# An mLSTM cell and a multiplicative FFN on one core: the division by the denominator on GpSimd, the output gate in one VectorE pass

## The chip, the cores and the metric

The kernel runs on 1 core of a Trainium2 chip. The core has five engines with a queue of instructions each: TensorE (PE in the profile; PEld are its weight loads), VectorE (DVE), ScalarE (ACT), GpSimd (POOL) and SyncE (SP, here used to issue DMAs). Each engine works through its own queue in order and waits on semaphores for the others. The metric is the device time of one execution in microseconds (us); lower is better.

## The reference

Two blocks follow each other, all in float32. The first is an mLSTM cell over 4 batches, 8 heads, 768 time steps and head size 40; the second is an FFN without an activation over the 3072 tokens.

```python
def _attn_ref(q, k, v, i_gate, f_gate, o_gate):
    ...
    for t in range(S):
        m_new = np.maximum(f_gate[:, :, t] + m, i_gate[:, :, t])
        f_stab = np.exp(f_gate[:, :, t] + m - m_new)
        i_stab = np.exp(i_gate[:, :, t] - m_new)
        m = m_new
        C = f_stab[:, :, None, None] * C + i_stab[:, :, None, None] * np.einsum('bhd,bhe->bhde', vt, kt)
        n = f_stab[:, :, None] * n + i_stab[:, :, None] * kt
        h_tilde = np.einsum('bhde,bhe->bhd', C, qt)
        nq = np.einsum('bhd,bhd->bh', n, qt)[:, :, None]
        denom = np.maximum(np.abs(nq), 1.0)
        o = 1.0 / (1.0 + np.exp(-o_gate[:, :, t]))
        y[:, :, t] = o * h_tilde / denom

def _moe_ref(x, w1, w2, w3, w_out):
    a = x @ w1
    b = x @ w2
    h = a * b @ w3
    return h @ w_out
```

The change touches the last line of the cell: `o * h_tilde / denom`.

## The kernel before

The cell is computed in chunks of 64 time steps. A unit is one batch and 128 time steps (two chunks) with all 8 heads; there are NU = 24 units, `n = 0..23`, four batches by six pairs of chunks, with time steps on the 128 partitions. For a unit, TensorE forms the scores `ss`, multiplies the masked weights `pw` with the values (`ph`), adds the part from the running state (`pi`), and makes the two state updates `pc`. A 41st column of the values is all ones, so column 40 of each head holds the denominator `nq`.

The main loop runs over steps `s = 0..31`. In step `s` the function `quarter_work(s, ...)` (from line 338) finishes the outputs of unit `s - 1` and starts unit `s`. Around it the same step puts in FFN work, so that TensorE always has something to do: the up products (`up`, `up_rest`: `pa`, `pb`, then `a_sb` and `ab`), in the first half the folding of the last two weight matrices into one (`convert`, `w3_mm`, `wp`), from step 19 on a seven-product scheme for the up products (`up_by_seven`) and later for the down products (`out_by_seven`).

The outputs of a unit are made in `outputs(n, pi, ph)` (line 420). VectorE first makes `h`, 8 heads by 41 columns per partition (L423 and, for units from 2 on, four instructions at L430). What follows is a Python generator of steps; each call of `den()` traces the next piece:

1. L438: the absolute value of column 40 into `den`, 128x8.
2. L440: maximum with 1, times 2.
3. L441: the reciprocal.
4. L443: `e = (e + 1) * den` over 128x320, where `e` is the tile `o_in`, which ScalarE has turned into tanh of half the output gate (`out_gate`, L270); L445: `y = h * e` over 128x320.

Since the sigmoid is (tanh(x/2) + 1) / 2 and `den` carries the 2, this is the reference's last line.

`quarter_work` places the calls between other VectorE work of unit `s`: after the mask of the scores (L397) come call 2, the first state update (L404, or L406 in the first four units), GpSimd's decay of the new state (L335, `decayed`), a late conversion in step 3 (`late`: L199, L200 of the weight `wr`), call 3, the second state update (L414, which reads what the decay wrote), and call 4. Units of the last pair of chunks (20 to 23) have one state update only, no second decay and no L414.

GpSimd's own queue has, per step, the decay L335, the weighting of the values `vw` for the next unit (L330), for part of the steps a copy of 64 columns of `y` (L476), two mask instructions on `pw` (L308) and the decay for the next unit (L335). In steps 16 and 17 it makes sums of weights (L659). From step 19 on it has two instructions of `up_by_seven`: L711, which finishes the set-aside sums that VectorE's L686 and L684 prepare and whose result the later L686 and L684 read, and L729, which multiplies the two factors into `ab`. From step 24 on L755 makes sums of the down weights.

From unit 15 on `y` is written to DRAM and read back in another layout by DMAs on SyncE's queue (L456, L458, L465), and VectorE turns it (L472) into the `xT` that the up products read; L666 makes the sums of `xT` that `up_by_seven` needs, and L770 the sums of `ab` for `out_by_seven`.

The order on TensorE is fixed as traced (`in_order`); that of the other engines too, from the first gate computation on, by `keep_order`, which links each instruction to the one traced before it on its engine. The `issue_after` blocks put what is traced in them behind the named instruction. The tiles `h`, `den` and `y` come from a pool with two buffers each, `a_sb` as well, and `o_in` has five.

Of the kernel before, what the change touches and what calls it, by code (L numbers as in the profile page):

```python
# [11 lines left out]
OP = mybir.AluOpType  # L12
# [4 lines left out]
def kernel(  # L17
# [26 lines left out]
    nc = tc.nc  # L44

    B, H, S, D = q.shape
    L = 64
    P = 128
# [6 lines left out]
    DM = H * D  # L55
# [21 lines left out]
    def mps(shape, name):  # L77
        pool = banks.pop(0)
        banks.append(pool)
        return pool.tile(shape, FP, name=name, tag="m")  # L80
# [10 lines left out]
    def mm(out, lhsT, rhs, start=True, stop=True):  # L91
        in_order(nc.tensor.matmul(out, lhsT=lhsT, rhs=rhs, start=start, stop=stop))  # L92
# [4 lines left out]
    def warm(n, m=4, small=0):  # L97
        bank = mps([P, 4, P], "fill")
        for _ in range(n):
            mm(bank[:, 0:m], ident, ident.unsqueeze(1).to_broadcast([P, m, P]))  # L100
        for i in range(small):
            r = halves[i % 2]
            mm(bank[r, 0, 0:L], ident[r, 0:L], ident[r, 0:L])
# [8 lines left out]
    N_DIAG = 2  # L112
# [154 lines left out]
    qT_t, kT_t, vw_t, before_t, y_t, x_t = {}, {}, {}, {}, {}, {}  # L267
# [65 lines left out]
    def decayed(new, old, n, x):  # L333
        c, b = divmod(n, B)
        nc.gpsimd.tensor_tensor(out=new, in0=old, op=OP.mult, in1=decay[:, b * NP:(b + 1) * NP, 2 * c + x:2 * c + x + 1]  # L335
                                .to_broadcast([P, NP, D1]))

    def quarter_work(s, rest, between, late):


        rest()

        def part(j, c0, n):
            return cell[j][:, :, c0:c0 + NP * n].rearrange("p x (n d) -> p x n d", d=n)

        ss, pc, pi = part(0, 0, L), part(0, NP * L, D1), part(1, 0, D1)
        ph = [cell[1][:, x, NP * D1:2 * NP * D1].rearrange("p (h d) -> p h d", d=D1) for x in range(2)]
        n = s - 1
        if 0 <= n < NU:
            pw, vt, qT = u_t.pop(n), vbuf[n % NBV], qT_t.pop(n)  # L350
            before = before_t.pop(n)
            if n < N_DIAG:
                warm(1)

            if n < N_DIAG:
                ph = mps([P, H, D1], "ph")
                for hq in range(H):
                    for r in halves:
                        mm(ph[r, hq, :], pw[r, hq, :], vt[r, hq, :])
            for hd in range(H // 2 if n >= N_DIAG else 0):  # L360
                for x, e in quarters:
                    hq = hd if x == e else hd + H // 2
                    mm(ph[x][halves[e], hd, :], pw[halves[x], hq, :], vt[halves[x], hq, :])
            for p in range(NP):
                for hip, x in quarters if n >= B else quarters[1:3]:
                    mm(pi[halves[x], hip, p, :], qT[heads[hip], p, halves[x]], before[x][heads[hip], p, :])
        den = None
        if 0 <= s - 1 < NU:
            den = outputs(s - 1, pi, ph)
            den()  # L370
            if between:
                for _ in range(3):
                    den()
                den = None
                between()
            if late:
                late()
        n, first_read = s, None
        if n < NU:
            c, b = divmod(n, B)  # L380
            kt, vw = kbuf[n % NB], vw_t.pop(n)
            ends = range(2 if c < NT2 - 1 else 1)
            first, second, after = state[b]
            before_t[n] = first, second
            state[b] = after, second, first
            kT, qT, pw = kT_t.pop(n), qT_t[n], u_t[n]
            for p in range(NP):
                for hip, x in quarters:
                    mm(ss[halves[x], hip, p, :], kT[heads[hip], p, halves[x]], qT[heads[hip], p, halves[x]])
            M = D if n else L  # L390
            for p in range(NP):
                for x, e in quarters:
                    if x in ends:
                        mm(pc[e * L:e * L + M, x, p, :], kt[halves[x], 2 * p + e, 0:M], vw[halves[x], 2 * p + e, :])
        if n < NU:
            pv = pw.rearrange("p (n two) t -> p two n t", two=2)
            first_read = nc.vector.tensor_tensor(out=pv, in0=ss, in1=pv, op=OP.mult)  # L397
        with tc.issue_after(first_read.ins) if first_read else nullcontext():
            if den:
                den()  # L400
            if n < NU:

                if c:
                    nc.vector.tensor_tensor(out=second, in0=pc[:, 0], in1=second, op=OP.add)  # L404
                else:
                    nc.vector.tensor_copy(out=second, in_=pc[:, 0])  # L406
                if len(ends) > 1:
                    decayed(after, second, n, 1)
            if late:
                late()  # L410
            if den:
                den()
            if n < NU and len(ends) > 1:
                nc.vector.tensor_tensor(out=after, in0=pc[:, 1], in1=after, op=OP.add)  # L414
            if den:
                done = den()
        return done if den else first_read

    def outputs(n, pi, ph):
        c, b = divmod(n, B)  # L420
        hs = slice(b * H, (b + 1) * H)
        h = sb.tile([P, H, D1], FP, name="h", tag="h")
        nc.vector.tensor_tensor(out=h.rearrange("p (n two) d -> p two n d", two=2), in0=pi,  # L423
                                in1=gT[:, c, hs].rearrange("p (n two) -> p two n", two=2).unsqueeze(3)
                                .to_broadcast([P, 2, NP, D1]), op=OP.mult)
        if n < N_DIAG:
            nc.vector.tensor_tensor(out=h, in0=ph, in1=h, op=OP.add)
        for x, e in quarters if n >= N_DIAG else ():
            part = h[halves[x], 0:H // 2] if x == e else h[halves[x], H // 2:H]
            nc.vector.tensor_tensor(out=part, in0=ph[x][halves[e]], in1=part, op=OP.add)  # L430

        den = sb.tile([P, H, 1], FP, name="den", tag="den")

        def steps():
            V = nc.vector
            yield V.tensor_scalar(out=den.bitcast(U32), in0=h[:, :, D:D1].bitcast(U32), scalar1=0x7FFFFFFF, scalar2=None,  # L438
                            op0=OP.bitwise_and)
            yield V.tensor_scalar(out=den, in0=den, scalar1=1.0, scalar2=2.0, op0=OP.max, op1=OP.mult)  # L440
            yield V.reciprocal(out=den, in_=den)  # L441
            e = o_t.pop(n)
            nc.vector.scalar_tensor_tensor(out=e, in0=e, scalar=1.0, in1=den.to_broadcast([P, H, D]), op0=OP.add, op1=OP.mult)  # L443
            y_t[n] = sb.tile([P, DM + REM], FP, name="y", tag="y")
            yield nc.vector.tensor_tensor(out=y_t[n][:, 0:DM].rearrange("p (h d) -> p h d", d=D), in0=h[:, :, 0:D],  # L445
                                           in1=e, op=OP.mult)

        done = steps()
        return lambda: next(done)

# [109 lines left out]
    V = nc.vector  # L560
# [7 lines left out]
    for i, r in enumerate(third):  # L568
        V.tensor_tensor_scan(out=M[r, 1:GC + 1], data0=F3[r, :, L - 1], data1=U3[r, :, L - 1], initial=M[r, 0:1],
                             op0=OP.add, op1=OP.max)  # L570
# [24 lines left out]
    for i, r in enumerate(third):  # L595
        nc.gpsimd.tensor_tensor(out=pick[r, :, i, :], in0=pair[r].to_broadcast([BH, B * NP, GC]), op=OP.mult,
                        in1=dec[r].unsqueeze(1).to_broadcast([BH, B * NP, GC]))
# [222 lines left out]
    for s in range(len(n_up)):  # L820
# [62 lines left out]
        def rest():  # L883
            for x in open_ups:
                up_rest(*x)
            if seven:
                seven[2]()
            if s == 3:
                scale_next()
                scale_next()  # L890

        def between():
            twice(1)
            weighted(2)
            rows_of_u(3)
            for _ in range(3):
                scale_next()
            for n in range(2):
                x_trans(n)
                if n == 0:  # L900
                    warm(1, small=38)
            for _ in range(3):
                convert()
            turn(2)
            block = up(*now[0])
            weighted(3)
            weights(3)
            masks(3)
            out_gate(2)
            convert()  # L910
            up_rest(*block)

        gated = None
        if s <= NU:
            gated = quarter_work(s, rest, between if s == 2 else None, convert if s == 3 else None)
        else:
            rest()
# [94 lines left out]
```

## Time and profile before

| what | value |
|---|---|
| median of 3 runs | 426.37 us (426.09 to 426.73) |
| span of the profiled execution | 425.8 us |
| ScalarE busy | 150.1 us (35%) |
| DMA traffic | 51.15 MB, mean 120 GB/s |
| L443, 24 instructions of 128x320 | 17.4 us, 0.725 us each |
| L445, 24 instructions of 128x320 | 17.0 us, 0.709 us each |
| L330, GpSimd, 24 of 128x328 | 18.3 us, 0.764 us each |
| L335, GpSimd, 40 of 128x164 | 20.0 us, 0.500 us each |
| L711 and L729, GpSimd, 22 each of 128x512 | 27.4 and 29.4 us |

The span is the time from the first to the last instruction of one profiled execution; the median is taken over separate runs and lies 0.6 us above it. Busy time is the time in which an engine works on an instruction; its waits are not in it. The granted TensorE clock is 0.996 of full speed over the span. In the rows of the timeline the first number is the start in us from the beginning of the span, the second the length, then the engine, the line, the operation, what is written and read, and the shape; a number in brackets is the idle time of that engine just before, with what ended it.

### The profile page before, as it was taken

To read this page: it belongs to the slowest core of one execution; us is meant where nothing else is said; L and a number is where in the kernel's file an instruction comes from. 1 tells how busy PE (TensorE), PEld (TensorE's weight loads), DVE (VectorE), ACT (ScalarE), POOL (GpSimd) and SP (SyncE) were. 2 spreads that over 40 slices of the span, in tenths; PEclk is the share of its full clock that TensorE was granted. 3 is DMA by queue.
4 is the path that set the end of the run, shared out by engine and by line. 5 is a ranking of instruction groups with operands and counts; after the bars stand their busy time and mean duration, and the time that the engine had idled before them with its cause. 6 is when DMAs were issued, how large, how long until landed. Compare 5 with 4: busy or idle time off the path is not lost.

```text
span 425.8 us, 13079 instructions
## 1 busy us (share of the span) xinstructions
PE 414.1 (97%) x5353; PEld 335.3 (79%) x5353; DVE 313.5 (74%) x635; ACT 150.1 (35%) x404; POOL 154.3 (36%) x211
## 2 busy tenths in 40 slices
PE   7989989999999999999999999999999999999996
PEld 4768878888688788787777778788778879888896
DVE  6676986888949779778736966596868699575971
ACT  4766865567723623630433313032311110210000
POOL 4421342233303303303307751546453587542100
PEclk9989999999999999999999999999999999999999
DMA  8999998598977776985425675756421120000001
GB/s 186 204 173 245 214 144 140 134 193 180 215 183 154 166 182 135 181 164 105 89 80 130 153 141 121 142 133 117 87 44 36 35 39 2 31 2 31 2 32 62
DMA packets 135211, 51.15 MB, mean 120 GB/s; under 512 B 109360, under 2 KB 126960, under 8 KB 135152
## 3 DMA queue, kind: packets, MB, share of 16 engines
q1 hardware_dynamic: 131552, 46.29, 53.9%
q10 hardware_dynamic: 3600, 4.03, 2.7%
q8 instruction: 42, 0.69, 0.7%
q14 instruction: 17, 0.14, 0.1%
HBM read 44.50 MB, written 5.80 MB: 118 GB/s over the span
## 4 chain that ended last, share of the span: by engine, by line
PE 53%; issue 20%; DVE 7%; POOL 7%; SPq 7%; DMA 5%; ACT 1%; POOLq 0%; DVEq 0%
PE cell L92 17%; PE pa L92 12%; PE o L92 8%; PE pb L92 8%; PE p L92 3%; POOL pw L308 3%; SPq L184 3%; DVE w3T L666 2%; PE pt L95 1%; POOL vw L330 1%; SPq L148 1%; DMA raw<-in_moe_w_dram 1%; PE fill L92 1%; POOL raw L659 1%; POOL state L335 1%
## 5 line engine op out<-in xcount | busy, mean ns | idle before, releaser
L335 POOL TENSOR_TENSOR state<-state,decay 128x164 f32<-128x164 f32 x40 | 20.0, 500 | 154.8 <-DVE state L404 129.0
L92 PE MATMUL pa<-xT,w 128*128 128x256 f32 x240 | 60.4, 382 | 0.0
L92 PEld LDWEIGHTS pa<-xT,w 128*128 128x128 f32 x240 | 44.4, 190 | 6.8 <-DVE h L430 0.4
L303 ACT ACTIVATE pw<-pw,aT 128x64 f32<-128x64 f32 x184 | 46.4, 339 | 3.2 <-ACT o_sb L741 1.9
L92 PE MATMUL pb<-xT,w 128*128 128x256 f32 x192 | 45.4, 379 | 0.0
L729 POOL TENSOR_TENSOR ab<-ab,a_sb 128x512 f32<-128x512 f32 x22 | 29.4, 1356 | 32.2 <-DVE ab L684 32.2
L92 PEld LDWEIGHTS pb<-xT,w 128*128 128x128 f32 x192 | 36.4, 190 | 5.0
L711 POOL TENSOR_TENSOR wo<-wo 128x512 f32<-128x512 f32 x22 | 27.4, 1268 | 29.8 <-DVE wo L686 29.8
L92 PE MATMUL pa<-xT,wr 64*64 64x256 f32 x384 | 37.0, 386 | 0.5 <-DVE wr L200 0.5
L92 PE MATMUL wp<-wo,w3T 128*128 128x320 f32 x128 | 35.9, 433 | 1.1 <-DVE ab L639 0.6
L308 POOL TENSOR_SCALAR_AFFINE_SELECT pw<-pw 64x512 f32<-64x512 f32 x48 | 35.8, 746 | 3.0 <-ACT pw L303 1.2
L92 PE MATMUL pb<-xT,wr 64*64 64x256 f32 x384 | 36.4, 380 | 0.0
L92 PE MATMUL cell<-w3o,ab 128*128 128x320 f32 x128 | 35.4, 432 | 0.0
L638 ACT ACTIVATE a_sb<-pa 128x512 f32<-128x512 f32 x24 | 14.3, 598 | 59.0 <-PE pb L92 59.0
L639 DVE TENSOR_TENSOR ab<-pb,a_sb 128x512 f32<-128x512 f32 x24 | 16.4, 688 | 23.2 <-ACT a_sb L638 22.8
L92 PEld LDWEIGHTS wp<-wo,w3T 128*128 128x128 f32 x128 | 23.8, 190 | 10.5 <-DVE ab L639 0.8
L92 PEld LDWEIGHTS cell<-w3o,ab 128*128 128x128 f32 x128 | 24.3, 190 | 9.5
L92 PEld LDWEIGHTS pa<-xT,wr 64*64 64x64 f32 x384 | 18.9, 132 | 15.4 <-issue 8.8
L686 DVE SCALAR_TENSOR_TENSOR a_sb<-pa,wo 128x512 f32<-128x512 f32 x12 | 8.3, 689 | 29.8 <-PE pa L92 29.8
L430 DVE TENSOR_TENSOR h<-cell,h 64x164 f32<-64x164 f32 x88 | 28.6, 326 | 1.6
L92 PE MATMUL po<-w3o,ab 128*128 128x320 f32 x96 | 26.4, 433 | 0.0
L92 PEld LDWEIGHTS po<-w3o,ab 128*128 128x128 f32 x96 | 18.1, 190 | 7.3
(180 smaller groups left out, 846.4 us busy)
## 6 DMA issues: line engine op xcount, KB each, us to landing
raw<-in_moe_w_dram SPq DMA_DIRECT2D x64, 128.0 KB, 3.4
kbuf<-in_k_dram SPq DMA_DIRECT2D x24, 160.0 KB, 4.5
v_all<-in_v_dram SPq DMA_DIRECT2D x24, 160.0 KB, 4.9
o_in<-in_o_gate_dram SPq DMA_DIRECT2D x24, 160.0 KB, 4.8
pw<-U_d SPq DMA_DIRECT2D x28, 128.0 KB, 3.5
raw<-in_moe_w_dram SPq DMA_DIRECT2D x5, 512.0 KB, 6.7
raw<-in_moe_w_out_dram SPq DMA_DIRECT2D x8, 320.0 KB, 4.1
gates<-in_k_dram SPq DMA_DIRECT2D x28, 80.0 KB, 2.5
```

What stands on the lines that cost most here:

```text
L92: in_order(nc.tensor.matmul(out, lhsT=lhsT, rhs=rhs, start=start, stop=stop))
L184: nc.sync.dma_start(out=dst, in_=src)
L303: nc.scalar.activation(out=pw[:, h, :], in_=src[:, h, :], func=AF.Exp, bias=aT[:, c, b * H + h:b * H + h + 1])
L308: nc.gpsimd.affine_select(out=pw[r], in_=pw[r], compare_op=OP.is_ge, fill=0.0, base=0, pattern=[[0, H], [1, L]], channel_multiplier=-1)
L335: nc.gpsimd.tensor_tensor(out=new, in0=old, op=OP.mult, in1=decay[:, b * NP:(b + 1) * NP, 2 * c + x:2 * c + x + 1] .to_broadcast([P, NP, D1]))
L430: nc.vector.tensor_tensor(out=part, in0=ph[x][halves[e]], in1=part, op=OP.add)
L638: nc.scalar.mul(out=a_sb, in_=pa, mul=UP ** -2)
L639: nc.vector.tensor_tensor(out=ab_t[gr][j][:, fs[0]:fs[-1] + 1, t0:t0 + a_sb.shape[-1]], in0=pb, in1=a_sb, op=OP.mult)
L666: nc.vector.tensor_tensor(out=dst, in0=p, in1=q, op=OP.subtract)
L686: nc.vector.scalar_tensor_tensor(out=out, in0=p, scalar=UP ** -2, in1=q, op0=OP.mult, op1=OP.add)
L711: aside_by.tensor_tensor(out=kept[j][:, 1:4:2], in0=kept[j][:, 1:3], in1=kept[j][:, 3:4].to_broadcast([128, 2, TH]), op=OP.add)
L729: aside_by.tensor_tensor(out=t[:, f:FO:FH, :], in0=t[:, f:FO:FH, :], in1=a, op=OP.mult)
```

## The change

For units 2 to 23 (`n >= N_DIAG`, and `N_DIAG` is 2) the two VectorE passes over 128x320 become one GpSimd pass and one VectorE pass. Right after the reciprocal GpSimd multiplies the first 40 columns of each head of `h` by the head's reciprocal, in place. VectorE's last pass is then `y = (e + 1) * h`. Units 0 and 1 keep the two VectorE passes. The tile `o_in` is no longer written by VectorE in the units that change.

In `quarter_work` the third call of `den()`, the reciprocal and with it GpSimd's multiply, moves for those units from behind the first state update, the decay and the late conversion to directly behind the second call. So on VectorE the reciprocal stands in front of L404 (or L406), and on GpSimd the multiply stands in front of the decay L335 of the same step; in steps 20 to 24, where the second decay is absent, it stands in front of the two L729. The instruction counts are 22 fewer on VectorE and 22 more on GpSimd; TensorE, ScalarE and SyncE have the same instructions in the same order. In the changed file L404 and L406 are L406 and L408, L414 is L416, L441 is L443, the new multiply is L452, the new last pass L454, and lines behind them are 8 higher.

```diff
@@ -398,6 +398,8 @@
         with tc.issue_after(first_read.ins) if first_read else nullcontext():
             if den:
                 den()
+                if s - 1 >= N_DIAG:
+                    den()
             if n < NU:
 
                 if c:
@@ -408,7 +410,7 @@
                     decayed(after, second, n, 1)
             if late:
                 late()
-            if den:
+            if den and s - 1 < N_DIAG:
                 den()
             if n < NU and len(ends) > 1:
                 nc.vector.tensor_tensor(out=after, in0=pc[:, 1], in1=after, op=OP.add)
@@ -438,12 +440,18 @@
...
-            yield V.reciprocal(out=den, in_=den)
+            done = V.reciprocal(out=den, in_=den)
             e = o_t.pop(n)
-            nc.vector.scalar_tensor_tensor(out=e, in0=e, scalar=1.0, in1=den.to_broadcast([P, H, D]), op0=OP.add, op1=OP.mult)
             y_t[n] = sb.tile([P, DM + REM], FP, name="y", tag="y")
-            yield nc.vector.tensor_tensor(out=y_t[n][:, 0:DM].rearrange("p (h d) -> p h d", d=D), in0=h[:, :, 0:D],
-                                           in1=e, op=OP.mult)
+            y, hn, all_d = y_t[n][:, 0:DM].rearrange("p (h d) -> p h d", d=D), h[:, :, 0:D], den.to_broadcast([P, H, D])
+            if n < N_DIAG:
+                yield done
+                V.scalar_tensor_tensor(out=e, in0=e, scalar=1.0, in1=all_d, op0=OP.add, op1=OP.mult)
+                yield V.tensor_tensor(out=y, in0=hn, in1=e, op=OP.mult)
+            else:
+                nc.gpsimd.tensor_tensor(out=hn, in0=hn, in1=all_d, op=OP.mult)
+                yield done
+                yield V.scalar_tensor_tensor(out=y, in0=e, scalar=1.0, in1=hn, op0=OP.add, op1=OP.mult)
```

## The prediction

> **What bounds the kernel now.** I read the busy line first, then the waits of TensorE, then the steps around the edited lines in order of time.
>
> ```profile
> PE 414.1 (97%) x5353; PEld 335.3 (79%) x5353; DVE 313.5 (74%) x635; ACT 150.1 (35%) x404; POOL 154.3 (36%) x211
> ```
>
> TensorE (PE) is busy for 414.1 of 425.8 us. VectorE (DVE) has a quarter of the span free, so taking work off it helps only where PE stands still for it. The waits of PE that end on a VectorE line this change can touch (us in total, times, longest):
>
> ```profile
> PE wp L92 <- DVE ab L639: 0.6, 1, 0.6
> PE pa L92 <- DVE wr L200: 0.5, 1, 0.5
> PE pa L92 <- DVE w3T L666: 0.4, 1, 0.4
> PE o L92 <- DVE wo L686: 0.2, 1, 0.2
> ```
>
> In time they lie at 107.8, 46.8, 242.4 and 355.9 us. Together 1.7 us: the most that relief of VectorE can return in the units that change (the wait for y at 22 us belongs to units 0 and 1, which keep their code). Now one ordinary unit, the end of step 17 (start, length, engine, line):
>
> ```profile
> 233.07 0.32 DVE L404 TENSOR_TENSOR state<-cell,state 128x164 f32<-128x164 f32 x1
> 233.31 0.20 DVE L441 RECIPROCAL den<-den 128x8 f32<-128x8 f32 x1
> 233.47 0.46 POOL L335 TENSOR_TENSOR state<-state,decay 128x164 f32<-128x164 f32 x1 [2.50 <-DVE state L404]
> 233.90 0.73 POOL L330 TENSOR_TENSOR vw<-v_all,wT 128x328 f32<-128x328 f32 x1
> 233.97 0.33 DVE L414 TENSOR_TENSOR state<-cell,state 128x164 f32<-128x164 f32 x1 [0.47 <-POOL state L335]
> 234.22 0.76 DVE L443 SCALAR_TENSOR_TENSOR o_in<-o_in,den 128x320 f32<-128x320 f32 x1
> 235.01 0.82 DVE L445 TENSOR_TENSOR y<-h,o_in 128x320 f32<-128x320 f32 x1
> ```
>
> VectorE already waits 0.47 us there for GpSimd's decay (L335). That queue is where the new multiply goes. Last, the step after the last unit (step 24) and the next:
>
> ```profile
> 335.68 2.50 POOL L729 TENSOR_TENSOR ab<-ab,a_sb 128x512 f32<-128x512 f32 x2 [4.06 <-DVE ab L684]
> ...
> 338.14 1.54 POOL L755 TENSOR_TENSOR v_all<-w3o 128x640 f32<-128x640 f32 x1
> 338.24 1.47 DVE L440 TENSOR_SCALAR den<-den 128x8 f32<-128x8 f32 x1
> 339.75 0.20 DVE L441 RECIPROCAL den<-den 128x8 f32<-128x8 f32 x1
> ...
> 342.40 2.50 POOL L711 TENSOR_TENSOR wo<-wo 128x512 f32<-128x512 f32 x2 [2.71 <-DVE wo L686]
> ...
> 343.71 0.69 DVE L686 SCALAR_TENSOR_TENSOR a_sb<-pb,wo 128x512 f32<-128x512 f32 x1
> ...
> 344.93 0.69 DVE L684 TENSOR_TENSOR ab<-pb,wo 128x512 f32<-128x512 f32 x1
> 345.07 2.94 POOL L729 TENSOR_TENSOR ab<-ab,a_sb 128x512 f32<-128x512 f32 x2 [0.17 <-DVE ab L684]
> ```
>
> From 336 to 356 us VectorE has no gap and the chain of waits runs on it (L440, L770, L472, L666, L686); at 356.12 PE's `o` product waits 0.22 us for the L686 that frees its bank. After that PE has no gap to the end. So whatever makes VectorE late here goes to the end one for one.
>
> **The change part by part.**
>
> Removed: in 22 units (2 to 23) VectorE's pass L443, mean 0.725 us, 16 us in all. Nearly all of it was behind a busy PE, so its worth is what the four waits lose, not 16 us.
>
> Added: 22 multiplies of 128x320 on GpSimd. No such row exists; the neighbours are L335 (164 columns, 0.46 us) and L330 (328 columns, 0.73), so a straight line gives 0.72 for 320. Bounds 0.46 and 1.25 (L729, 512 columns). They need the reciprocal and are queued in front of the decay L335.
>
> Ordinary units, steps 4 to 19, worked on the rows above: the reciprocal now stands before L404 and ends at about 233.4; multiply 233.45 to 234.2; L335 to 234.6; L414 starts at 234.65 (before 233.97); y to 235.7, counting 0.76 to 0.82 for a pass beside GpSimd. It ended at 235.83. So VectorE swaps a pass for a wait and gains 0.1 us; GpSimd is 0.7 us later with vw, the mask and what follows. Hidden by: vw and mask are needed a step later (10 us in the later steps, about 1 us for vw in step 3).
>
> Step 3 (unit 2): the reciprocal now stands in front of L406 and the conversion of `wr` (L199, L200) instead of behind them. That is its 0.19 us and a gap of 0.03, and PE waits for just that L200: **+0.2** (0.1 to 0.4).
>
> The wait at 107.8: y of step 8 ended at 99.6, but L199 then waited 0.63 us for ScalarE, so an earlier y is no help; GpSimd's mask slides some 0.3 us further over L199, L200 and the transpose, of which L199 took 0.62 beside the mask and 0.39 alone: **+0.1** (-0.1 to 0.3).
>
> The wait at 242.4: step 17's four L666 run beside GpSimd's L659 (1.12, 1.38, 1.49) and only the last ran nearly free (0.68). GpSimd 0.7 us later puts that last one beside L659 as well, about +0.5; y earlier gives 0.15 back. **+0.3** (-0.4, the whole wait gone, to 0.6).
>
> Steps 19 to 23: the multiply is ahead of the products L729 in the queue, and it needs the reciprocal, so L729 goes from 307.42 to about 311.6 in step 22 (reciprocal 310.75, plus 0.1, plus 0.72), likewise in 20, 21 and 23. What waits behind it: vw, mask, decay, the next L711 and PE's `cell` products of the third group, which read the finished `ab` from 313.5. First half of L729 then ends at 312.9 to 313.2: cover 0.3 to 0.6 us at least, more because the columns in question are read fourth. L711 of step 23 slides from 315.66 to about 317; its reader, L686 into a_sb at 320.18, still has room. **0** (0 to 0.5; past the cover each us costs one).
>
> Steps 24 and 25: the two L729 and the L755 now come after the multiply. L755 then no longer sits beside L440, which shrinks from 1.47 to 0.16; reciprocal ends at 338.6, multiply 338.7 to 339.4, L729 to 342.15 (2.74 for the pair, as beside VectorE's two passes in step 19), L755 to 343.7. L711 of step 25 begins there instead of at 342.40. VectorE is no earlier for it: y runs beside L729, where L445 took 1.44 in step 19, and ends near 340.8 against 341.00. L686 and L684 need the halves of L711, so L684 at 344.93 and the four L770, L472, L666 and L686 behind it all move by **+1.3**. Bounds: 0.8 (multiply at 0.46, L729 2.50, L755 1.54), 1.9 (L729 2.94, L755 1.98); and -0.2 if the pair kept its place, for then only the 0.22 us wait is left to win.
>
> [...] This case has 0.73 us for L330's 328 columns against 0.49 for an undisturbed L445 of 320, a factor of 1.5. [...]
>
> [...]
>
> Sum: 0.2 + 0.1 + 0.3 + 0 + 1.3 = 1.9 us on the profiled span of 425.8, which is 0.6 below the median of the runs (426.37); the sum is carried to the median: 428.2 to 428.3, I say **428.2**.
>
> **The rivals.**
>
> *No change to be told (about 0.2% is what a measurement of this kernel can tell).* PE covers the tail too: if the scheduler's banks give PE's `o` product at 356 some 1 us of room the trace doesn't show, only steps 3 and 17 remain, +0.3: 426.7. For it: PE has 97% and no gap between 243 and 355.9. Against it: at 356.12 PE already waits.
>
> *Faster.* VectorE's freed 16 us take away the waits at 107.8, 242.4 and 355.9 (0.58 + 0.41 + 0.22 = 1.2) less 0.2 in step 3: 425.4. One mechanism: in steps 17 and 24 a shorter VectorE chain arrives earlier; at step 24 1.3 us of L440 beside L755 vanish. It decides if GpSimd finishes L755 before 342.4, so that L711 starts when L686 lets it. Against it: 338.7 + 0.46 + 2.50 + 1.54 is already 343.2.
>
> *Much slower.* The products L729, some 4 us later in steps 20 to 23, outrun their cover at 313.5 or hold up L711: up to 2 us more, 430.2. For it: half a us of cover by my rows; against it: the columns are read fourth, 1.6 us into the block.
>
> **How the numbers follow.** Forecast 0.60, no change 0.19, faster 0.11, much slower 0.10. Faster by over 0.2%: 0.11; within: 0.19; slower: 0.70. The terms' bounds run from 0.4 (0.1 - 0.1 - 0.4 + 0 + 0.8) to 3.7 (0.4 + 0.3 + 0.6 + 0.5 + 1.9), that is 426.8 to 430.1; taking in the case of no change and its scatter the range is 426.2 to 430.1.
>
> **What would show it.** In the changed profile: the multiply near 0.72 us, 22 times; L414's wait of 0.47 grown to about 1.0; VectorE's busy time down by some 14 us at a span not shorter; L729 of steps 20 to 23 begun after the reciprocal; L711 of step 25 waiting for no VectorE row but for its own queue; PE's wait at 356 grown from 0.2 to about 1.5. I am wrong if that last wait is not longer, or if PE shows a new gap in 243 to 350.

## The result and the profile after

| | before | after |
|---|---|---|
| median (lowest to highest, runs) | 426.27 us (426.09 to 426.73, 4) | 428.47 us (428.27 to 429.39, 4) |
| time after / before, 95% interval | | 1.0063 [1.0044, 1.0082] |
| span of the profiled execution | 425.8 us | 426.4 us |

The changed kernel is slower by 1.9 to 3.5 us (the interval's ends, 0.0044 and 0.0082, times 426.27); the quotient of the two medians, 1.0052, lies within. A run more than 1.5% above the fastest of its kernel counts as slow and is left out of the ratios and of the ranges of runs given below. The spans alone would say 0.6 us, and that is misleading: wherever span and time of one execution are both known they lie 1.9 to 2.1 us apart (after: 426.4 and 428.45), so the profiled execution of before took about 427.8 us and was not a typical one.

The busy line of the page after, to be read against the one of before:

```profile
PE 413.1 (97%) x5353; PEld 334.6 (78%) x5353; DVE 303.8 (71%) x613; ACT 149.6 (35%) x404; POOL 169.4 (40%) x233
```

VectorE is busy 9.7 us less (313.5 to 303.8), GpSimd 15.1 us more. PE's own work is the same within 1.0 us. So the answer must be in the waits of PE, in the same view as before (total, times, longest, in us):

```profile
PE o L92 <- DVE wo L694: 1.4, 1, 1.4
PE pa L92 <- DVE wr L200: 1.3, 1, 1.3
...
PE cell L92 <- DVE state L416: 0.7, 2, 0.4
PE wp L92 <- DVE ab L647: 0.7, 1, 0.7
PE pa L92 <- DVE w3T L674: 0.6, 1, 0.6
```

Four of the five grew from 0.2, 0.5, nothing and 0.4; the one for `ab` stood at 0.6. Each has its place. First step 3 in the timeline of after (start, length, engine, line):

```profile
44.36 0.20 DVE L443 RECIPROCAL den<-den 128x8 f32<-128x8 f32 x1
44.64 0.72 POOL L452 TENSOR_TENSOR h<-h,den 128x320 f32<-128x320 f32 x1 [8.26 <-DVE den L443]
44.67 0.97 DVE L199 TENSOR_SCALAR wr<-raw 128x512 uint32<-128x512 uint32 x1
45.78 0.73 DVE L200 CUSTOM_DVE_ANT_0 wr<-raw,wr 128x1024 uint16<-128x1024 uint16 x1
46.57 0.43 PE L92 MATMUL pa<-xT,wr 64*64 64x256 f32 x1 [1.31 <-DVE wr L200]
```

The same place in the timeline of before:

```profile
45.99 0.42 DVE L199 TENSOR_SCALAR wr<-raw 128x512 uint32<-128x512 uint32 x1
46.54 0.73 DVE L200 CUSTOM_DVE_ANT_0 wr<-raw,wr 128x1024 uint16<-128x1024 uint16 x1
47.33 0.43 PE L92 MATMUL pa<-xT,wr 64*64 64x256 f32 x1 [0.51 <-DVE wr L200]
```

L199 starts 0.03 us after the new multiply and takes 0.97 us instead of 0.42. PE waits 0.8 us longer for what follows it.

Second, the ordinary units, in the timeline of after: the end of step 17, then of step 18.

```profile
231.45 0.72 POOL L452 TENSOR_TENSOR h<-h,den 128x320 f32<-128x320 f32 x1 [1.94 <-DVE den L443]
232.13 0.47 POOL L335 TENSOR_TENSOR state<-state,decay 128x164 f32<-128x164 f32 x1
232.55 0.74 POOL L330 TENSOR_TENSOR vw<-v_all,wT 128x328 f32<-128x328 f32 x1
232.63 0.33 DVE L416 TENSOR_TENSOR state<-cell,state 128x164 f32<-128x164 f32 x1 [1.06 <-POOL state L335]
232.87 0.76 DVE L454 SCALAR_TENSOR_TENSOR y<-o_in,h 128x320 f32<-128x320 f32 x1
...
243.94 0.72 POOL L452 TENSOR_TENSOR h<-h,den 128x320 f32<-128x320 f32 x1 [2.70 <-DVE den L443]
244.62 0.47 POOL L335 TENSOR_TENSOR state<-state,decay 128x164 f32<-128x164 f32 x1
245.12 0.33 DVE L416 TENSOR_TENSOR state<-cell,state 128x164 f32<-128x164 f32 x1 [1.07 <-POOL state L335]
...
245.50 0.70 PE L92 MATMUL cell<-w3T,raw 128*128 128x256 f32 x2 [0.38 <-DVE state L416]
```

The decay L335 stands behind the multiply, L416 waits 1.06 us for it (0.47 before). In step 17 nobody minds. In step 18 the next PE product writes the PSUM bank that L416 still reads (`pc`), and PE stands still for 0.38 us; the same in step 19 at 264.5 us (0.33). Before, the PE products ran through there: 

```profile
245.78 0.46 POOL L335 TENSOR_TENSOR state<-state,decay 128x164 f32<-128x164 f32 x1 [3.29 <-DVE state L404]
...
246.28 0.33 DVE L414 TENSOR_TENSOR state<-cell,state 128x164 f32<-128x164 f32 x1 [0.47 <-POOL state L335]
246.39 2.32 PE L92 MATMUL cell<-w3T,raw 128*128 128x256 f32 x10
```

Third, the tail, steps 24 and 25, in the timeline of after:

```profile
338.09 0.72 POOL L452 TENSOR_TENSOR h<-h,den 128x320 f32<-128x320 f32 x1 [7.09 <-DVE den L443]
338.77 2.75 POOL L737 TENSOR_TENSOR ab<-ab,a_sb 128x512 f32<-128x512 f32 x2
338.85 1.54 DVE L454 SCALAR_TENSOR_TENSOR y<-o_in,h 128x320 f32<-128x320 f32 x1 [0.84 <-POOL h L452]
...
341.48 1.54 POOL L763 TENSOR_TENSOR v_all<-w3o 128x640 f32<-128x640 f32 x1
...
342.98 2.50 POOL L719 TENSOR_TENSOR wo<-wo 128x512 f32<-128x512 f32 x2
...
344.29 0.69 DVE L694 SCALAR_TENSOR_TENSOR a_sb<-pb,wo 128x512 f32<-128x512 f32 x1 [1.25 <-POOL wo L719]
...
356.71 1.35 PE L92 MATMUL o<-w3o,ab 128*128 128x160 f32 x8 [1.43 <-DVE wo L694]
```

GpSimd works without a pause from 338.09; multiply, two products, L763, and only then L719, for which VectorE now waits 1.25 us. Before, L719 (as L711) had waited for VectorE instead. PE's wait 12 us later is 1.2 us longer.

Laid side by side, matmul by matmul, the two traces give the account. At 59 us the profiled execution of after is 2.5 us ahead. That of before had lost 1.0 us in small waits up to 23 us, 1.6 us in a slow stretch of PE at 23 to 28 us and 1.7 us at 57.6 us, in a gap that ends on no other engine; that of after 0.9 us at 43 us (it waited for `w`) and 0.9 us at 47 us. From there after falls back by 0.4 us at 108 and 144 us, where the other kernels differ from before by as much in either direction, then by 0.2 at the wait for `w3T`, 0.6 at each of the two `cell` products and 1.2 at 356 us, and it ends 0.6 us behind. With the 0.9 us at 47 us that the early lead covers, the places that touch the change sum to 3.5 us, the upper end of the measured interval.

### The profile page after: what moved, and what is told of

It reads as the page before. It is cut to its first block, busy times and chain, and to the rows that moved or that the text cites. A ratio compares the mean times of both kernels' runs of the same rounds, so it can differ in the third digit from the quotient of the medians.

```text
span 426.4 us, 13083 instructions
## 1 busy us (share of the span) xinstructions
PE 413.1 (97%) x5353; PEld 334.6 (78%) x5353; DVE 303.8 (71%) x613; ACT 149.6 (35%) x404; POOL 169.4 (40%) x233
## 4 chain that ended last, share of the span: by engine, by line
PE 77%; SPq 8%; DVE 6%; DMA 5%; issue 3%; POOL 1%; ACT 0%; DVEq 0%; POOLq 0%
PE cell L92 19%; PE pa L92 19%; PE pb L92 12%; PE wp L92 8%; PE o L92 8%; PE po L92 4%; SPq L139 3%; PE p L92 3%; DMA raw<-in_moe_w_dram 2%; SPq L184 2%; PE px L95 1%; DVE pw L778 1%; PE pt L95 1%; SPq L153 1%; DMA v_all<-in_v_dram 1%
## 5 line engine op out<-in xcount | busy, mean ns | idle before, releaser
L452 POOL TENSOR_TENSOR h<-h,den 128x320 f32<-128x320 f32 x22 | 15.9, 724 | 172.8 <-DVE den L443 172.8
L737 POOL TENSOR_TENSOR ab<-ab,a_sb 128x512 f32<-128x512 f32 x22 | 30.7, 1416 | 13.9 <-DVE ab L692 13.9
L308 POOL TENSOR_SCALAR_AFFINE_SELECT pw<-pw 64x512 f32<-64x512 f32 x48 | 34.3, 715 | 1.8 <-ACT pw L303 0.2
L719 POOL TENSOR_TENSOR wo<-wo 128x512 f32<-128x512 f32 x22 | 27.5, 1272 | 11.9 <-DVE wo L694 11.9
L694 DVE SCALAR_TENSOR_TENSOR a_sb<-pa,wo 128x512 f32<-128x512 f32 x12 | 8.3, 689 | 29.3 <-PE pa L92 29.2
```

The lines of the kernel that those rows point to most:

```text
L308: nc.gpsimd.affine_select(out=pw[r], in_=pw[r], compare_op=OP.is_ge, fill=0.0, base=0, pattern=[[0, H], [1, L]], channel_multiplier=-1)
L452: nc.gpsimd.tensor_tensor(out=hn, in0=hn, in1=all_d, op=OP.mult)
L719: aside_by.tensor_tensor(out=kept[j][:, 1:4:2], in0=kept[j][:, 1:3], in1=kept[j][:, 3:4].to_broadcast([128, 2, TH]), op=OP.add)
L737: aside_by.tensor_tensor(out=t[:, f:FO:FH, :], in0=t[:, f:FO:FH, :], in1=a, op=OP.mult)
```

## The experiments

All times are medians in us, ratios are against the kernel before, run on the same chip in the same batch. Its own median was 425.64 for the first four kernels (23 runs, 424.5 to 427.4), 426.05 for the next four (23 runs, 424.4 to 430.3) and 426.44 for the last four (24 runs, 424.7 to 428.9). Single executions scatter by more than the effects, so each kernel was also read by PE's waits in its profile. The table has both; waits in us: for `wr` at 46, for `w3T` at 242, for L416 in steps 18 and 19 (two), and in the tail.

| kernel | time | ratio, 95% interval | wr | w3T | L416 | tail |
|---|---|---|---|---|---|---|
| before (profile shown) | | | 0.51 | 0.41 | none | 0.22 |
| after (profile shown) | 428.47 | 1.0063 [1.0044, 1.0082] | 1.31 | 0.59 | 0.38, 0.33 | 1.43 |
| only the last unit changed | 427.46 | 1.0046 [1.0025, 1.0067] | 0.55 | 0.42 | none | 1.44 |
| all but the last unit | 428.74 | 1.0079 [1.0050, 1.0109] | 1.31 | 0.59 | 0.37, 0.32 | 0.25 |
| new order, old passes | 428.65 | 1.0068 [1.0043, 1.0093] | 0.75 | 0.62 | none | 0.22 |
| multiply behind the decay | 429.22 | 1.0073 [1.0044, 1.0101] | 0.75 | 1.15 | none | 1.43 |
| sums of step 24 moved to 25 | 430.27 | 1.0122 [1.0079, 1.0164] | 1.27 | 0.97 | 0.37, 0.32 | 1.46 |
| repaired | 426.63 | 1.0020 [0.9996, 1.0043] | 0.51 | 0.41 | none | 0.21 |
| after, again | 431.47 | 1.0128 [1.0097, 1.0160] | 1.31 | 0.65 | 0.37, 0.33 | 1.42 |
| before, again | 426.57 | 1.0014 [0.9985, 1.0043] | 0.55 | 0.41 | none | 0.22 |
| unit 2 the old way | 429.41 | 1.0076 [1.0043, 1.0110] | 0.61 | 0.96 | 0.36, 0.32 | 1.40 |
| only unit 2 changed | 427.99 | 1.0040 [1.0013, 1.0067] | 1.30 | 0.40 | none | 0.22 |
| sum of step 24 moved to 23 | 430.23 | 1.0089 [1.0067, 1.0112] | 0.39 | 0.96 | 0.37, 0.32 | 0.20 |
| repaired, sum in step 23 | 426.32 | 1.0014 [0.9990, 1.0039] | 0.55 | 0.56 | none | none |

**Only the last unit changed.** A function says which units keep the old code; here all but unit 23.

```diff
+    def old_way(n):
+        return n != 23
...
-                if s - 1 >= N_DIAG:
+                if not old_way(s - 1):
...
-            if den and s - 1 < N_DIAG:
+            if den and old_way(s - 1):
...
-            if n < N_DIAG:
+            if old_way(n):
```

> Only unit 23 gets the GpSimd multiply, units 0 to 22 keep the two VectorE passes. Tail theory (the multiply holds the two L737 and the first L763 of step 24 back, so L719 of step 25 starts late): PE's wait for the o product near 355 us grows from 0.2 to 1.4, the waits at 245 and 265 of the changed kernel are absent, time 1.2 us above the kernel before, some 427.5. Rival (loss is spread over all units): the tail wait stays near 0.2, time within 0.4 of before.

The view of PE's waits for this kernel (its lines lie 3 higher than in after, L697 is L694):

```profile
PE o L92 <- DVE wo L697: 1.4, 1, 1.4
...
PE pa L92 <- DVE wr L200: 0.5, 1, 0.5
PE pa L92 <- DVE w3T L677: 0.4, 1, 0.4
```

One multiply out of 22 makes the whole tail wait (1.44 us) and leaves every other wait as it was before. The time rises by 1.1 to 2.9 us by the interval; the wait gives 1.2.

**All but the last unit.** The same with another condition.

```diff
     def old_way(n):
-        return n != 23
+        return n < N_DIAG or n == 23
```

> Units 2 to 22 as in the change, unit 23 keeps the two VectorE passes. Tail theory: the wait at 355 is back at 0.2, the waits of PE on the second state update (L416) in steps 19 and 20 stay at 0.3 to 0.4 each with a drift of 0.5 to 0.6 each; time 1.2 below the change, about 427.2. Rival (spread over all units): time stays within 0.3 of the change, 428.2.

The tail wait is back at 0.25, the others are those of after. The time did not fall below that of after: 428.74, 2.1 to 4.6 us over before, where the remaining waits give 2.1. The two kernels together place 1.2 us of wait in unit 23, but this time does not confirm the saving.

**New order, old passes.** The reciprocal stands early for all units from 2 on, but VectorE does both passes and GpSimd no multiply.

```diff
-            if n < N_DIAG:
+            if True:
```

> The reciprocal stands early as in the change, but units 2 to 23 keep both passes on VectorE and GpSimd multiplies nothing. If the place of the reciprocal in front of the wr conversion costs: PE's wait for wr near 46 us is 0.2 longer and the time 0.2 above before (426.5). If the engine's queue is the cost: time equal to before within 0.3, no wait on L416 in steps 19 and 20, tail wait 0.2.

The wait for `wr` is 0.75, and L199 takes its 0.42 us: the early reciprocal costs 0.2 of the 0.8, the rest needs the multiply beside L199. L416 and the tail are untouched. The time (+1.8 to +4.0 us) is far more than the 0.4 us that these waits explain. In the profile the kernel also waits 1.2 us for `w` at 43.7 us and 1.8 at 57.5 us, which vary between executions of one and the same kernel (0.8 and 1.3, 0 and 2.0 in the two profiles of after). The first of them ends before the reciprocal's new place (L443 at 45.56 us here), so the new order can't be its cause; for the second that stays open.

**Multiply behind the decay.** Instead of the third call of `den()` the fourth issues it, after `decayed`; the reciprocal stays early.

```diff
                     decayed(after, second, n, 1)
+            if den and s - 1 >= N_DIAG:
+                den()
...
-                nc.gpsimd.tensor_tensor(out=hn, in0=hn, in1=all_d, op=OP.mult)
                 yield done
+                yield nc.gpsimd.tensor_tensor(out=hn, in0=hn, in1=all_d, op=OP.mult)
```

> As the change, but GpSimd runs the decay L335 before the multiply, so the second state update waits 0.5 us again instead of 1.06, while y starts at the same time. Bank theory (PE's waits at 245 and 265 us are for the score bank that the late second state update still reads): both waits go, time 1.1 below the change, about 427.3; the tail wait of 1.4 stays, since step 24 has no decay. Rival (those waits come from VectorE or GpSimd being late in general): they stay, time 428.4.

Step 18 in its timeline (L455 is the multiply, L418 the second state update):

```profile
245.33 0.46 POOL L335 TENSOR_TENSOR state<-state,decay 128x164 f32<-128x164 f32 x1 [3.49 <-DVE state L406]
...
245.73 2.47 PE L92 MATMUL cell<-w3T,raw 128*128 128x256 f32 x10
245.75 0.72 POOL L455 TENSOR_TENSOR h<-h,den 128x320 f32<-128x320 f32 x1
245.82 0.33 DVE L418 TENSOR_TENSOR state<-cell,state 128x164 f32<-128x164 f32 x1 [0.57 <-POOL state L335]
```

PE runs its products through again: the two waits for L416 come from the queue order of multiply and decay. Matmul by matmul, what follows these two places falls behind before by 0.64 and 0.59 us in after and by 0.15 and 0.10 us here, so the queue order is worth 0.5 us each; the rest comes with the early reciprocal, for the kernel with the old passes has it too. L199 is at 0.42 us and the wait for `wr` at 0.75, as with the old passes. The tail, which has no decay, is as in after. The wait for `w3T` is 1.15 in this execution, in which VectorE waited 0.80 us for the DMA that brings `yb` (0.28 in after). The time is not below that of after.

**Sums of step 24 moved to step 25.** L763 is taken out of the queue ahead of L719.

```diff
-            for _ in range({NU: 1, NU + 1: 3}.get(s, 0)):
+            for _ in range({NU + 1: 4}.get(s, 0)):
```

> The changed kernel with one move: the down-weight sum of step 24 (L763, 1.54 us) is issued in step 25 behind its two L737, with the other three. Tail theory: L719 of step 25 starts when VectorE's L694 lets it and no longer behind L763, PE's wait near 355 us falls from 1.43 to 0.3 or less; the waits for wr (1.3) and on L416 (0.3 to 0.4, twice) stay; time about 1.2 below the changed kernel. Rival (the tail is late because y is late): the wait stays above 1.

The timeline of this kernel, steps 25 and 26:

```profile
342.42 2.50 POOL L719 TENSOR_TENSOR wo<-wo 128x512 f32<-128x512 f32 x2 [0.27 <-DVE wo L694]
...
353.84 1.73 POOL L763 TENSOR_TENSOR q_all<-w3o,gates 128x640 f32<-128x640 f32 x1
354.19 1.65 DVE L674 TENSOR_TENSOR w3T<-xT,w3T 128x256 f32<-128x256 f32 x1
...
357.36 1.35 PE L92 MATMUL o<-w3o,ab 128*128 128x160 f32 x8 [1.46 <-DVE wo L694]
```

L719 waits for VectorE again and not for its own queue, as meant. But the last L763 now lies beside a L674, which takes 1.65 us instead of 0.43. The 1.2 us moved 12 us down the same VectorE chain. The expected gain failed to come, though L719 does wait as expected.

**Repaired.** Units 2, 16 and 23 the old way, the others with the multiply behind the decay: 19 passes of VectorE fewer than before.

```diff
+    def old_way(n):
+        return n <= N_DIAG or n in (16, 23)
...
+            if den and not old_way(s - 1):
+                den()
...
```

> Units 0 to 2, 16 and 23 as before the change; for the others GpSimd multiplies, but behind the decay. If the ledger of PE waits is whole: wr wait 0.5, no waits on L416, wait for w3T 0.4, tail wait 0.2, so PE waits as in the kernel before, and the time is within 0.4 of before although VectorE does 19 passes less. Rival (the GpSimd multiplies cost beside VectorE everywhere): time 2 us above before, as in the changed kernel.

All four waits are at their size before (0.51, 0.41, none, 0.21), and the time is that of before within its interval (-0.2 to +1.8 us). So with these waits gone no loss is left that this measurement can tell, and what is left of the change, 19 passes, is worth nothing that can be measured. These 19 units have the early reciprocal as well, so outside units 2, 16 and 23 it costs nothing that can be measured either.

**After and before, again**, unaltered, in the same batch.

> The changed kernel again, for a second trace and times on the chip of these runs. Ledger theory: the waits of PE are again 1.3 (wr), 0.6 (w3T), twice 0.3 to 0.4 (L416) and 1.4 (tail), and the time is 2.2 to 3.4 above before. Rival (part of them is chance of one execution): one or more of these waits is absent or differs by more than 0.2.

> The kernel before again, as a control: waits of PE 0.5 (wr), 0.4 (w3T), none on L414, 0.2 (tail); ratio 1.000 within its interval. If the slow stretch at 24 to 27 us and the gap of 1.5 at 57 us are chance, they may be absent here and the span lies up to 3 us lower; if they belong to the kernel they are there again.

Before against itself gave 1.0014. After came out at 431.47, 4.1 to 6.8 us over before, with the same waits to 0.1 us as in its first profile. In the first batch the same kernel was 1.9 to 3.5 us over before, and the two intervals don't overlap: they hold within a batch, and between batches the time of a kernel is certain to some 3 us only. What follows of single terms therefore rests on the waits, not on the times. Its profiled execution (span 430.5) had also 1.27 us of wait for `w` at 43 us, 2.03 at 57.6 and a slow stretch of PE at 59 to 61 us. Against the first profile these add 0.5, 2.0 and some 1.2 us, most of the 4.1 us between the two spans; the change's own waits add 0.1.

**Unit 2 the old way, and only unit 2 changed.** Two conditions for the same function.

```diff
+    def old_way(n):
+        return n <= N_DIAG
...
```

> The changed kernel with unit 2 left as before (late reciprocal, two VectorE passes). Ledger theory: the wait for wr is 0.5 again, the waits on L416 (0.3 to 0.4, twice) and the tail wait (1.4) stay; time some 2.5 above before, 0.8 below the changed kernel. Rival (unit 2's new order costs far more than its wait, since the kernels with it measured 1 to 2 above their ledgers): time 1.5 or less above before.

```diff
+    def old_way(n):
+        return n != N_DIAG
...
```

> Only unit 2 is changed. Ledger theory: wr wait 1.3, L199 of wr 0.97 us beside the multiply instead of 0.42, all other waits as before, time 0.8 above before. Rival (unit 2's order costs more than its wait): time 1.5 to 3 above before.

The wait for `wr` is 0.61 without and 1.30 with unit 2's new code, and nothing else was changed in the second of the two kernels, so unit 2 makes it. The times, +3.0 (1.8 to 4.7) and +1.5 (0.6 to 2.9), agree with the sums of the waits, about 3.0 and 0.8. That the order in unit 2 also worsens the waits at 43 and 57 us is not shown: both kernels had 1.3 us at 43, and the one at 57 was 0.5 and 1.5.

**Sum of step 24 moved to step 23.** The other way out of the tail: L763 earlier.

```diff
-            for _ in range({NU: 1, NU + 1: 3}.get(s, 0)):
+            for _ in range({NU - 1: 1, NU + 1: 3}.get(s, 0)):
```

> The changed kernel with the first down-weight sum (L763, 1.54 us) issued one step earlier, in step 23 behind its two L737, where GpSimd is idle for some us, so nothing is moved onto the later passes. Tail theory: L719 of step 25 waits for VectorE again, L674 stays at 1.16 and 0.43, PE's wait near 355 falls from 1.43 to 0.3 or less; the other waits as in the change; 1.2 below it. Rival (any placing of that sum costs VectorE as much): the wait stays near 1.4.

In its timeline, where the kernel with the sums moved to step 25 had 1.46:

```profile
343.86 2.49 POOL L719 TENSOR_TENSOR wo<-wo 128x512 f32<-128x512 f32 x2 [0.27 <-DVE wo L694]
...
355.63 0.43 DVE L674 TENSOR_TENSOR w3T<-xT,w3T 128x256 f32<-128x256 f32 x1
...
357.57 1.35 PE L92 MATMUL o<-w3o,ab 128*128 128x160 f32 x8 [0.20 <-DVE wo L694]
```

Here the tail wait is gone although GpSimd still does the multiply of unit 23: what matters is whether L763 stands between it and L719. The time is no lower than that of after. The profile holds 2.01 us of waiting for ScalarE's `qT` at 39 us, which other kernels have at 0 to 0.5; it does not explain the other runs. Two of the other waits are not those of after: 0.96 for `w3T`, and only 0.39 for `wr`. In this execution L199 itself waited 0.55 us for ScalarE and began 0.66 us after the multiply, when that was nearly done, and took 0.43 us. So the long wait for `wr` is not in every execution of the new code.

**Repaired, sum in step 23.** Both edits together.

> Units 0 to 2, 16 and 23 as before, the others with the multiply behind the decay, and the first down-weight sum in step 23. The lock of L440 behind that sum (1.47 instead of 0.16 us) goes, VectorE is 1.3 us ahead from 339 on, PE's tail wait 0.2 falls to 0; PE waits 0.2 less than in the kernel before. Time 0.0 to 0.4 below before, too little to be told for sure. Rival (a shorter VectorE chain is worth more): more than 1 us below before.

The L763 beside the denominators of step 24 is gone, the maximum takes 0.17 us instead of 1.47, and PE does not wait in the tail at all (0.22 before). The time is that of before (-0.4 to +1.7 us). The 0.2 us is less than this measurement sees, and no kernel here is shown to be faster than before.

## Why the prediction was right

The time, 428.2 predicted and 428.47 measured, and the direction were right. The largest term, the tail, was right in mechanism and size. The sum as a whole was not: predicted 1.9 us in five terms, shown by the waits 3.3 us (0.8 + 0.2 + 1.1 + 1.2) in four places, of which two were wrong in size or missing. That the time came within 0.3 us is luck: the right terms would have given 429.7, and the same kernel measured 431.47 in a later batch.

- **The tail, +1.3.** Right in place, mechanism and size: PE's wait went from 0.22 to 1.43, L719 started at 342.98 behind L763 (338.1 + 0.72 + 2.75 + 1.54, with overlaps), and the kernel with only this unit changed shows it alone. The multiply took the 0.72 us of the straight line.
- **Step 3, +0.2.** Right place, wrong size. The step "that is its 0.19 us and a gap of 0.03" counted only what the move puts ahead of L199. The kernel with the old passes confirms those 0.2. It forgot that the multiply then runs beside L199, which costs 0.55 more; the same paragraphs had priced such neighbours at 107.8 and 242.4.
- **The wait at 242.4, +0.3.** Mechanism right: the last of the four passes now lies beside GpSimd (1.49 instead of 0.68 us) while the first is free (0.42). Measured +0.2 in three profiles of kernels with unit 16 changed (after, after again, all but the last unit). It was +0.55 to +0.74 in four others, where the `yb` that VectorE turns first landed 0.66 to 0.84 us after VectorE was free, not 0.26 to 0.34; there the four passes take about what they took before (1.01 to 1.20, 1.38, 1.49, 0.68) and only begin later. How late `yb` lands varies without the change too (0.93 us and a wait of 0.56 in a kernel with unit 16 the old way), so the part that is shown to be the change's is +0.2.
- **The wait at 107.8, +0.1.** It is 0.58 before and 0.40 to 0.85 in the others, 0.69 with its unit unchanged. No effect is shown.
- **Ordinary units, nothing.** This step failed. It followed GpSimd's queue to `vw` and the mask and let "VectorE swap a pass for a wait" in L414. It named L414's wait, 0.47 growing to about 1.0 (measured 1.06), but did not ask who waits for L414: in steps 18 and 19 it is PE, whose next product takes the bank. Two gaps, of 0.38 and 0.33 us, set the later matmuls back by 0.6 us each, 0.5 of it from the queue order. The sign given for being wrong, a new gap of PE between 243 and 350, did come.
- **Steps 19 to 23, nothing.** L737 did start after the reciprocal (310.97 in step 22, from 307.42), and PE waited for it nowhere. The cover held.
- **VectorE's busy time.** 9.7 us less, not 14: the remaining pass L454 takes 0.964 us on average, 0.76 beside `vw` and 1.54 in the tail, where L445 took 0.709.
- **Carried to the median.** The step that put the span 0.6 us under the median failed: span and time differ by 2.0 us, so the profiled execution of before was 1.4 us slower than the median. It left the sum unharmed only because the sum was of differences.

Of the rivals, "no change" gave PE 1 us of room at 356 us; there is none. (Its sum was off as well: the terms of steps 3 and 17 are 0.2 and 0.3, which makes 426.9, not 426.7.) "Faster" needed L763 done before 342.4; it was done at 343.0. "Much slower" had L729 outrun its cover; it did not: times of 430 and more came up in later batches, but no profile has a wait of PE on L737.

What stays open: the measured times lie above the sum of the waits in most kernels, by 0.6 us even for before against itself, and for the new order alone, for after in its second batch and for the sum in step 23 by more than their intervals allow. The profiles of these put the rest into the first 60 us, where waits for data and for the conversions of weights vary in every kernel. The wait for `w` at 43 us ends before the first instruction that the change touches (L443 at 44.36 us in after), so the change's order can't cause it. The gap at 57.6 us stands in four of the eight profiles with unit 2's new code (1.5 to 2.0 us) and in four of the six with its old code (0.5 to 1.5 us); so few traces can't tell whether the change makes it larger. What the rest of the time comes from is open.

## What to carry to other kernels

Ask first what the bounding engine waits for the engine that is relieved: here 16 us of VectorE passes removed bought nothing, and PE had waited 1.7 us in all. When an instruction is put into a queue ahead of others, follow what stands behind it to its readers, and then ask who reuses the buffer that those readers hold: here L416 waited 1.06 us for the decay instead of 0.47, and PE stood still for 0.38 and 0.33 us for the PSUM bank that L416 was reading. And before moving work from VectorE to GpSimd, list what will run beside it at the two or three places without slack; L199 beside the multiply took 0.97 us instead of 0.42.

## What the runs showed of the hardware

Some VectorE passes that met a GpSimd instruction were not slowed by a share; they ended as if they had waited for its end. Four pairs of rows above and in the prediction fit one sum: end of the GpSimd instruction, plus the pass's own time alone, less 0.14 to 0.15 us.

| pass, alone | beside | GpSimd ends | sum | measured end |
|---|---|---|---|---|
| L199, 0.42 | L452, 0.72 | 45.36 | 45.78 | 45.64 |
| L454, 0.49 (as L445) | L330, 0.74 | 233.29 | 233.78 | 233.63 |
| L674, 0.42 | L763, 1.73 | 355.57 | 355.99 | 355.84 |
| L440 before, 0.17 | L755, 1.54 | 339.68 | 339.85 | 339.71 |

So even a pass over 8 columns took 1.47 us (L440). Other passes kept their time. Those with an operand in PSUM did; in the profiles of before and after none of them took over 0.02 us longer beside GpSimd than the longest of its kind alone: L694 took 0.69 us beside L719 as elsewhere (344.29), L416 0.33 beside L330 (232.63). So did some that stay within SBUF: in after the transpose L480 took its usual 0.56 us at 352.97, inside an L763 that ran from 352.46 to 354.45, while the L674 right behind it took 1.16 instead of 0.42; in before the reciprocal L441 took its 0.19 us at 47.20, inside an L330 that ran from 46.69 to 47.87.

L454 and L674 read two tensors in SBUF and waited; L416, L694, L480 and L441 read one and did not. The number of inputs in SBUF alone doesn't tell the passes apart, for L199 and L440, with one input each, waited in the rows of the table. What does is not shown.

The other surprise is the scatter: runs of the unaltered kernel before lay between 424.4 and 430.3 us, while its first four spread over 0.6 us. A narrow spread of a few runs was no measure of it.
